# Backward pass of an attention and gated feed-forward block: one fixed use for each PSUM bank in the heads, places recomputed, and nine heads that make dV and dK in their stored layout

## Chip, core and metric

The kernel runs on one core of one Trainium2 chip. The metric is the device time of an execution in microseconds. A core has five engines that the text calls by these names: TensorE (PE in the profile; PEld is its weight load), VectorE (DVE), ScalarE (ACT), GpSimd (POOL) and SyncE (SP). Each engine works through its own instructions in order; matmuls write to PSUM, which has eight banks of 128 partitions x 512 f32 values. PSUM is emptied by VectorE or ScalarE. GpSimd and SyncE also issue the DMAs.

## The reference

The reference returns the output of a forward pass and its gradients (a vector-Jacobian product with grad_out). The forward pass, with S = 2048 rows, D = 576, 32 heads of size 128, F = 4608, all in bfloat16:

```
xn  = layernorm(x)
q   = (xn @ wq) by heads
p   = softmax(q @ k_cache^T / sqrt(128))        per head, 2048 x 2048
s   = concat_heads(p @ v_cache) @ wo
h   = sigmoid(xn @ w_gate) * (xn @ w_up)
g   = silu(h @ w_down)
out = x + s * g
```

Nine results are returned: out, dx, dK (out_2) and dV (out_3) of every head, dwq, dwo, dw_gate, dw_up, dw_down. For a head, with dO the gradient of its output, P the probabilities and delta the row sums of dO * O: dV = P^T dO, dS = P * (dO V^T - delta), dQ = dS K, dK = dS^T Q (with scales). dK and dV of a head are 2048 x 128.

## The kernel before

The kernel has stages that follow each other: layer norm and the feed-forward forward pass (to about 310 us), the down projection (to about 470 us), the 32 heads (to about 3680 us), the output projection (L851), the first feed-forward backward pass over 18 blocks of 256 of F's columns (L906 to L961), the gradients of wo and wq over 8 groups of heads (L1006, L1017), and the gradient of x (L1075).

**A head's work on TensorE.** The query rows come in 16 tiles (qt) of 128. For each qt and each half of the keys there are two 512-wide matmuls for the scores (s_half, L553) and later two for dP (dp_half, L586). VectorE takes the scores out with a running minimum (L555), ScalarE makes the unnormalised probabilities P (s_exp, L565), VectorE and ScalarE make dS (L589, L592, L596). SyncE issues transposing DMAs of pairs of P and dS tiles (trans_P, trans_dS). Then come the rows: for every qt 16 matmuls, 128 wide, of the transposed P with V (O, 256 per head) and of the transposed dS with K (dQ, 256 per head). Four qt make a group that fills one PSUM bank (row_mm, L617). A group of O is copied by ScalarE (o_sink: ou) and goes on to GpSimd (prod, o_n) and VectorE (delta); a group of dQ is copied by VectorE (dq_sink: dq_n, L680).

dV and dK are made in four passes per head (kv, kv_mm, L635): VA and VB give the halves of dV, KA and KB those of dK. A pass has 32 matmuls, 512 wide, and fills two banks with the result turned, head size on the partitions: the weights are a tile of dOn or Qn, the moving operand is a slab of P or dS. Each bank is copied by ScalarE (KVE = "ss") and stored by a GpSimd DMA to the scratch tensors dvT_d and dkT_d. dOn is the transposed dO, scaled in pairs of tiles by the reciprocal row sums (s_rinv on VectorE, s_scale on GpSimd, L573) once the exps of the pair are done; the first dV pass needs it.

Projections (proj, L510; 20 matmuls for QT of the next head, 20 for dOT) and transposes (pe_transposes, L517, in two groups of 8 each for KT, VT, dOn, Qn; prep_wo, five) fill one bank each and are copied by ScalarE or VectorE.

**Order.** A head has 64 places (HEAD). Every call is put into a list with a place by at(); the score and dP matmuls are anchors at the whole places (scores in 0 to 31, dP in 32 to 63). The list is sorted by place, and TensorE, VectorE and ScalarE get their instructions in that order. GpSimd's and SyncE's order is chosen when the kernel is built. Rows of group g start at place 13.6 + 8g (O) and 45.6 + 8g (dQ) and fill 8 places, so that groups follow each other directly; the places of the dV and dK passes come out of level(), which fills the places up to an equal load. They are 23.2 to 36.0 (VA), 37.4 to 53.2 (VB), 54.6 to 66.5 (KA) and 67.9 to 84.9 (KB); places over 64 lie in the next head.

**PSUM.** Score and dP matmuls use a pool of two buffers of two banks (ps_big). All else in the heads, rows, dV and dK passes, projections and transposes, shares one pool of four banks (ps_acc, tag "acc").

**Turns.** After the heads, dkT_d and dvT_d have to be turned: turn() issues on SyncE's queue a transposing DMA of 512 KB into SBUF and stores the tile that the turn before it brought (L156, L159). There are 64, one for each of dK and dV of each head: one in each block of the first feed-forward backward pass and one more in each odd block (27), two in each group of the next stage (16), and three in each of the last seven of eight blocks of the last (21).

Of the kernel before, what the change touches and what calls it, by code (L numbers as in the profile page):

```python
# [13 lines left out]
P = 128  # L14
# [81 lines left out]
def kernel(  # L96
# [47 lines left out]
    on2_d = dram.tile([S, HD], bf, name="on2_d")  # L144
    dq2_d = dram.tile([S, HD], bf, name="dq2_d")
    dkT_d = dram.tile([H, P, S], bf, name="dkT_d")
    dvT_d = dram.tile([H, P, S], bf, name="dvT_d")
    turns = [(src[h], out[0, h].rearrange("(p t) d -> p t d", t=NT)) for h in range(H) for src, out in ((dkT_d, out_2), (dvT_d, out_3))]
    turned = []
# [271 lines left out]
    with tc.tile_pool(name="ld2", bufs=2) as ld2, tc.tile_pool(name="ld1q", bufs=1) as ld1q, \  # L421
# [8 lines left out]
            tc.tile_pool(name="wh", bufs=2) as wh, tc.tile_pool(name="ld1", bufs=1) as ld1, \  # L430
            tc.tile_pool(name="ps_acc", bufs=4, space=PSUM) as ps_acc:

# [59 lines left out]
        def prep_wo(hs, eng):  # L492
            hs.woT = wh.tile([P, DT, P], bf, name="woT_h", bufs=1)
            nc.gpsimd.memset(hs.woT[:P - KL, DL, :], 0.0)
            pt = ps_acc.tile([P, 8, P], bf, name="acct", tag="acc")
            for j in range(DL):
                nc.tensor.transpose(pt[:, j, :], wo_h[:, j * P:(j + 1) * P], ident[:])
            nc.tensor.transpose(pt[:, DL, :], wo_h[:, D - P:D], ident[:])
            alt.copy(hs.woT[:, :DL, :], pt[:, :DL, :], eng=eng)
            alt.copy(hs.woT[P - KL:, DL, :], pt[P - KL:, DL, :], eng=eng)  # L500

        def proj(hs, name, c, i, eng):
            if c == 0 and i == 0:
                setattr(hs, name, ld1.tile([P, S], bf, name=name))
            w, srcT = (hs.wq, xnT) if name == "QT" else (hs.woT, dsT)
            cs = slice(c * CH, (c + 1) * CH)
            if i == 0:
                hs.acc_ = ps_acc.tile([P, CH], f32, name="accp", tag="acc")
            acc = hs.acc_
            nc.tensor.matmul(acc[:], lhsT=w[:, i, :], rhs=(srcT if i < DL else xnT)[:, i, cs], start=(i == 0), stop=(i == DL))  # L510
            if i == DL:
                alt.copy(getattr(hs, name)[:, cs], acc[:], eng=eng)

        def pe_transposes(src_fn, dst, g, eng):
            pt = ps_acc.tile([P, 8, P], bf, name="acct", tag="acc")
            for j in range(8):
                nc.tensor.transpose(pt[:, j, :], src_fn(g * 8 + j), ident[:])  # L517
            alt.copy(dst[:, g * 8:(g + 1) * 8, :], pt[:], eng=eng)
# [94 lines left out]
        def row_mm(bx, hs, T, rhs, qt, kt, sink):  # L613
            j = qt % GQ
            if j == 0 and kt == 0:
                bx.acc = ps_acc.tile([P, GQ, P], f32, name="acc", tag="acc")
            nc.tensor.matmul(bx.acc[:, j, :], lhsT=T[qt][:, kt, :], rhs=getattr(hs, rhs)[:, kt, :],  # L617
                             start=(kt == 0), stop=(kt == NT - 1))
            if j == GQ - 1 and kt == NT - 1:
                sink(bx.acc)  # L620

        def rows(pos, step, width, hs, T, rhs, g, sinks):
            bx = Box()
            sink, after = sinks
            for j in range(GQ):
                for kt in range(NT):
                    at(pos + step * j + width * kt / NT, row_mm, bx, hs, T, rhs, g * GQ + j, kt, sink)
            if after:
                at(pos + step * (GQ - 1) + width + AFTER, after)

        def kv_mm(bx, hs, slabs, rhs, half, qt, i, sink):
            if qt == 0:
                bx.acc[i] = ps_acc.tile([P, CH], f32, name="acckv", tag="acc")
            k0 = (half * 2 + i) * CH
            nc.tensor.matmul(bx.acc[i][:], lhsT=getattr(hs, rhs)[:, qt, :], rhs=slabs[qt][:, k0:k0 + CH],  # L635
                             start=(qt == 0), stop=(qt == NT - 1))
            if qt == NT - 1:
                sink(bx.acc[i], i)

        def kv(b, pos, hs, slabs, rhs, half, dst):  # L640
            bx = Box()
            bx.acc = [None, None]

            def sink(acc, i):
                c = half * 2 + i
                kv_t = stg.tile([P, CH], bf, name="kv", tag="stg", bufs=3)
                alt.copy(kv_t[:], acc[:], eng=KVE[i])
                nc.gpsimd.dma_start(dst[:, c * CH:(c + 1) * CH], kv_t[:])

            n = 2 * KPC  # L650
            for qt in range(NT):
                for i in range(2):
                    at(b + pos[qt * n + i * KPC], kv_mm, bx, hs, slabs, rhs, half, qt, i, sink)

# [31 lines left out]
        HEAD = 2 * H1  # L686
        XO, XQ = 13.6, 13.6
        KVE, OUE = "ss", "s"
        WOT_AT = 1.6
        QT_AT, DOT_AT = ((39.0, 47.2, 50.2, 56.4), "s"), ((7.8, 10.4, 16.2, 18.6), "s")  # L690
        KT_AT, DON_AT, VT_AT, QN_AT = (42.0, 43.6, "s"), (14.9, 24.4, "v"), (3.4, 26.4, "s"), (28.0, 32.2, "s")
        PSTEP = 0.4
        EXP_AT, RINV_AT, PT_AT, DST_AT, AFTER = 2.1, 4.6, 2.7, 2.0, 3.5

        KV0, KV1, GAP = 23.2, 85.9, 1.1
        BLK, WIDE = 1.0, CH / P
        load_ = [2 * WIDE + NT / 2] * (2 * HEAD)
        for p_ in (WOT_AT,):
            load_[int(p_)] += DT
        for ps_, n_ in [((KT_AT + DON_AT + VT_AT + QN_AT), 8)]:  # L700
            for p_ in ps_:
                if not isinstance(p_, str):
                    load_[int(p_)] += n_ * BLK
        for p_ in QT_AT[0] + DOT_AT[0]:
            for i in range(DT):
                load_[int(p_ + PSTEP * i)] += WIDE
        for k in range(HEAD):
            load_[HEAD + k] = load_[k]

        def level(top):  # L710
            out, pos, n = [], KV0, 2 * KPC * NT
            while pos < 2 * HEAD - 1 and len(out) < 4 * n:
                if len(out) % n == 0 and out:
                    pos += GAP
                k = int(pos)
                room = max(top - load_[k], 0.01)
                step = 1.0 / room
                out.append(pos)
                pos = min(pos + step, max(k + 1.0, pos + 1e-6)) if step > k + 1.0 - pos else pos + step
                if len(out) < n and len(out) % (2 * KPC) == 0:  # L720
                    pos = max(pos, 4.0 * (len(out) // (4 * KPC)) + 7.0)
            return out, pos

        lo_, hi_ = 10.0, 60.0
        for _ in range(60):
            mid = (lo_ + hi_) / 2
            o_, e_ = level(mid)
            if len(o_) < 4 * 2 * KPC * NT or e_ > KV1:
                lo_ = mid
            else:  # L730
                hi_ = mid
        kvpos = level(hi_)[0]
        assert len(kvpos) == 4 * 2 * KPC * NT
        VA, VB, KA, KB = (kvpos[2 * KPC * NT * k:2 * KPC * NT * (k + 1)] for k in range(4))
        WO_AT = 50.0
        MAN = {mybir.EngineType.PE, mybir.EngineType.DVE, mybir.EngineType.Activation}
        for h in range(H):
            hs = Head(h)
            b = h * HEAD
            back = lambda x: b - HEAD + x if h else b - 14 + x / 8  # L740
            at(back(35.0), load_w, hs)
            at(back(35.1), load_kv, hs)
            for c in range(NCH):
                for i in range(DT):
                    at(back(QT_AT[0][c] + PSTEP * i), proj, hs, "QT", c, i, QT_AT[1])
                    at(b + DOT_AT[0][c] + PSTEP * i, proj, hs, "dOT", c, i, DOT_AT[1])
            at(b + WOT_AT, prep_wo, hs, "s")
            for g in range(2):
# [17 lines left out]
            for g in range(NG):  # L766
                rows(b + 8 * g + XO, 2, 2, hs, hs.PT, "Vn", g, o_sink(hs, g))
                rows(b + H1 + 8 * g + XQ, 2, 2, hs, hs.dST, "Kn", g, dq_sink(hs, g))
            for half, (pv, pk_) in enumerate(((VA, KA), (VB, KB))):
                kv(b, pv, hs, hs.P, "dOn", half, dvT_d[h])  # L770
                kv(b, pk_, hs, hs.dS, "Qn", half, dkT_d[h])
        bl = (H - 1) * HEAD
# [15 lines left out]
    if True:  # L788
# [79 lines left out]
        FB = min(256, F)  # L868
        with tc.tile_pool(name="b1o", bufs=2, reuse_waits="tile") as outp, tc.tile_pool(name="b1k", bufs=3, reuse_waits="tile") as tkp, tc.tile_pool(name="b1t", bufs=3, reuse_waits="tile") as tmpp, \
                tc.tile_pool(name="b1r", bufs=2, reuse_waits="tile") as dblk, \  # L870
# [20 lines left out]
            for fb in range(F // FB):  # L891
                if fb % 2:
                    turn(tkp)
                fcols = slice(fb * FB, (fb + 1) * FB)
# [147 lines left out]
        with tc.tile_pool(name="c4c", bufs=1, reuse_waits="tile") as chp, tc.tile_pool(name="c4s", bufs=2, reuse_waits="tile") as sb, \  # L1042
# [11 lines left out]
            for sbi in range(S // SB2):  # L1054
# [7 lines left out]
                for pi, (src_d, wT, k0, KC, nm) in enumerate(passes):  # L1062
                    ch = chp.tile([P, KC, SB2], bf, name=f"cq{pi % 2}" if nm == "cq" else f"cf{pi % 3}")
                    nc.sync.dma_start_transpose(ch[:], src_d[scol, k0 * P:(k0 + KC) * P])
                    if sbi == 0 and pi in (1, 3, 4, 6):
                        load_wqT((1, 3, 4, 6).index(pi))
                    elif sbi and pi % 3 == 1:
                        turn(tkp)
# [67 lines left out]
```

## Time and profile before

| | us |
|---|---|
| three timed runs | 5139.92, 5182.06, 5144.55 |
| median of these | 5144.55 |
| the profiled execution, its own time | 5156.55 |
| its span, first to last instruction | 5154.8 |
| one head, from one wait of TensorE to the same wait in the next (1977.44 to 2077.06) | 99.6 |

| busy in a stretch of 100 us | TensorE | VectorE | ScalarE | GpSimd |
|---|---|---|---|---|
| 2000 to 2100 us (heads) | 96.8 | 81.7 | 64.5 | 32.9 |
| 4100 to 4200 us (first feed-forward backward pass) | 88.2 | 24.7 | 19.6 | 27.7 |
| 4900 to 5000 us (gradient of x) | 99.2 | 12.6 | 3.6 | 4.3 |

A view of the profile is of one execution. A line of the timeline gives the start, the duration, the engine, the line of the kernel, the operation with its operands (written <- read), the shapes, how many like it were merged, and in brackets the idle time before it with what ended it. A line of the view of waits gives who waited for whom, the total, how often, and the longest. Some matmul records are missing from the trace. Matmuls are pipelined: the next starts before the last has ended, so the issue rate is read from start to start.

### The profile page before, as it was taken

The page shows a single profiled execution, that of the slowest core. Times are in us where ns is not written, and L with a number is a line of the kernel's source. Part 1 is how long each engine was busy: PE and PEld are TensorE (multiplying, and loading weights), DVE is VectorE, ACT ScalarE, POOL GpSimd, SP SyncE. Part 2 cuts the span into 40 slices and gives each one's busy share as a digit, 9 for nine tenths or more (in the row PEclk, how much of TensorE's full clock was granted, in tenths as well). Part 3 has the DMA queues.
Part 4 walks back from the last instruction along what each step waited for, and adds up shares of the span by engine and source line. Part 5 has one row for each costly group of instructions (what it writes and reads, how often), then busy time and mean ns, then how long its engine had stood idle before and what let it go on. Part 6 is the DMA issues. An engine that isn't in the chain of part 4 may idle for free.

```text
span 5154.8 us, 100626 instructions
## 1 busy us (share of the span) xinstructions
PE 4926.1 (96%) x41765; PEld 3051.4 (59%) x42512; DVE 3157.1 (61%) x4789; ACT 2415.2 (47%) x3099; POOL 1479.5 (29%) x2197
## 2 busy tenths in 40 slices
PE   9999999999999999999999999999888999998999
PEld 3344666666666666666666566666547778754554
DVE  6545888888888888888888788888432222110101
ACT  5533656666665665666666566656201222100000
POOL 4322332332333333233333323332212233211000
PEclk9999999999999999999999999999999999999999
DMA  7876999999999999999999999999999999999998
GB/s 263 256 210 149 202 208 201 204 207 201 206 202 204 204 204 206 205 203 205 207 202 202 199 202 204 204 202 217 201 208 224 223 242 239 281 266 242 208 206 183
DMA packets 2905211, 1095.60 MB, mean 213 GB/s; under 512 B 2710064, under 2 KB 2832944, under 8 KB 2904752
## 3 DMA queue, kind: packets, MB, share of 16 engines
q1 hardware_dynamic: 2819488, 803.33, 87.4%
q0 software_dynamic: 85264, 285.79, 20.4%
q8 instruction: 332, 5.44, 0.4%
q14 instruction: 127, 1.04, 0.1%
HBM read 172.54 MB, written 234.55 MB: 79 GB/s over the span
## 4 chain that ended last, share of the span: by engine, by line
PE 76%; DMA 7%; issue 6%; DVE 5%; ACT 5%; POOL 1%; SPq 1%; ACTq 0%; DVEq 0%; POOLq 0%; another core or an unknown queue 0%
PE acc L617 14%; PE acckv L635 13%; PE acc L1075 8%; PE dp L586 7%; PE sp L553 6%; PE accp L510 5%; PE accw L948 4%; DVE sneg L555 3%; PE acc L391 3%; PE dh L906 2%; PE accd L924 2%; PE acc L1006 2%; PE accq L1017 2%; DMA b_blk<-b_d 2%; PE acc L851 2%
## 5 line engine op out<-in xcount | busy, mean ns | idle before, releaser
L565 ACT ACTIVATE Pq<-sneg,nm 128x2048 bf16<-128x2048 bf16 x512 | 1026.7, 2005 | 158.9 <-DVE sneg L555 156.2
L617 PE MATMUL acc<-Kn,dST 128*128 128x128 bf16 x8192 | 1034.5, 219 | 28.3 <-DMA dST<-dSq 16.7
L589 DVE SCALAR_TENSOR_TENSOR dSq<-dp,delta,Pq 128x1024 bf16<-128x1024 f32 x608 | 773.2, 1281 | 378.8 <-PE dp L586 377.2
L617 PEld LDWEIGHTS <-dST 128*128 128x128 bf16 x8192 | 713.8, 98 | 466.8 <-issue 28.0
L617 PE MATMUL acc<-Vn,PT 128*128 128x128 bf16 x8192 | 947.3, 219 | 30.1 <-ACT dOT L40 15.5
L617 PEld LDWEIGHTS <-PT 128*128 128x128 bf16 x8192 | 680.2, 98 | 417.0 <-issue 25.4
L635 PE MATMUL acckv<-dSq,Qn 128*128 128x512 bf16 x1915 | 707.5, 380 | 23.1 <-ACT kv L40 22.1
L635 PE MATMUL acckv<-Pq,dOn 128*128 128x512 bf16 x1892 | 701.0, 380 | 26.5 <-POOL dOn L573 22.8
L555 DVE TENSOR_SCALAR_CACHE_REDUCE sneg<-sp 128x1024 bf16<-128x1024 f32 x512 | 625.4, 1222 | 143.6 <-PE sp L553 90.8
L555 DVE TENSOR_SCALAR_CACHE_REDUCE sneg<-sp,nm 128x1024 bf16<-128x1024 f32 x512 | 656.8, 1283 | 74.2 <-PE sp L553 48.0
L592 ACT ACTIVATE t<-dp,negdelta 128x1024 bf16<-128x1024 f32 x416 | 464.2, 1116 | 454.4 <-PE dp L586 288.7
L553 PE MATMUL sp<-KT,QT 128*128 128x512 bf16 x1985 | 597.9, 380 | 7.0 <-DVE sneg L555 6.7
L586 PE MATMUL dp<-VT,dOT 128*128 128x512 bf16 x1913 | 580.4, 379 | 1.8 <-DVE dSq L589 1.0
L596 DVE TENSOR_TENSOR dSq<-t,Pq 128x1024 bf16<-128x1024 bf16 x416 | 407.4, 979 | 0.0
L635 PEld LDWEIGHTS <-dOn 128*128 128x128 bf16 x2048 | 200.6, 98 | 99.0 <-POOL dOn L573 34.6
L1088 DVE SCALAR_TENSOR_TENSOR junk<-dxn,xn_all 128x576 f32<-128x576 f32 x16 | 12.1, 758 | 381.3 <-ACT dxn L1083 381.3
L510 PE MATMUL accp<-xnT,wq_h 128*128 128x512 bf16 x639 | 241.2, 382 | 3.5 <-ACT xnT L40 0.8
L635 PEld LDWEIGHTS <-Qn 128*128 128x128 bf16 x2048 | 200.7, 98 | 72.7
L948 PEld LDWEIGHTS <-xn_all 128*128 128x128 bf16 x2304 | 224.1, 98 | 30.6 <-issue 2.8
L1075 PEld LDWEIGHTS <-cf 128*128 128x128 bf16 x2304 | 147.6, 99 | 154.3 <-DMA cf<-du_d 7.5
L573 POOL TENSOR_TENSOR dOn<-dOn,rinv_all 128x256 bf16<-128x256 bf16 x256 | 153.9, 610 | 204.8 <-DVE rinv_all L569 147.0
L1083 ACT ACTIVATE dxn<-acc 128x512 f32<-128x512 f32 (+1 forms) x32 | 12.8, 406 | 413.6 <-issue 344.3
(182 smaller groups left out, 6983.4 us busy)
## 6 DMA issues: line engine op xcount, KB each, us to landing
out_dram<-turn SPq DMA_DIRECT2D x64, 512.0 KB, 4.5
h_d<-h_row POOLq DMA_DIRECT2D x48, 384.0 KB, 3.0
a_d<-a_row POOLq DMA_DIRECT2D x48, 384.0 KB, 3.4
b_d<-b_row POOLq DMA_DIRECT2D x48, 384.0 KB, 4.5
a_blk<-a_d SPq DMA_DIRECT2D x18, 1024.0 KB, 13.2
b_blk<-b_d SPq DMA_DIRECT2D x18, 1024.0 KB, 18.9
du_d<-du_blk POOLq DMA_DIRECT2D x18, 1024.0 KB, 9.4
dg_d<-dg_blk POOLq DMA_DIRECT2D x18, 1024.0 KB, 12.8
```

The lines of the kernel that those rows point to most:

```text
L510: nc.tensor.matmul(acc[:], lhsT=w[:, i, :], rhs=(srcT if i < DL else xnT)[:, i, cs], start=(i == 0), stop=(i == DL))
L553: nc.tensor.matmul(sp[:, c * CH:(c + 1) * CH], lhsT=hs.QT[:, qs], rhs=hs.KT[:, hf * HW_ + c * CH: hf * HW_ + (c + 1) * CH], start=True, st ...
L555: nc.vector.tensor_scalar(sneg[:, hf * HW_:(hf + 1) * HW_], sp[:], -SCALE, None if hf == 0 else nm[:, hf - 1:hf], op0=ALU.mult, op1=ALU.mi ...
L565: nc.scalar.activation(Pq, sneg[:], AF.Exp, bias=nm[:, hf:hf + 1], scale=-1.0, accum_out=hs.rs_all[:, qt:qt + 1])
L586: nc.tensor.matmul(dp[:, c * CH:(c + 1) * CH], lhsT=hs.dOT[:, qs], rhs=hs.VT[:, hf * HW_ + c * CH: hf * HW_ + (c + 1) * CH], start=True, s ...
L589: nc.vector.scalar_tensor_tensor(dSq[:, hsl], dp[:], hs.delta[:, qt:qt + 1], Pq[:, hsl], op0=ALU.subtract, op1=ALU.mult)
L592: nc.scalar.activation(t[:], dp[:], AF.Identity, bias=hs.negdelta[:, qt:qt + 1], scale=1.0)
L596: nc.vector.tensor_tensor(dSq[:, hsl], t[:], Pq[:, hsl], op=ALU.mult)
L617: nc.tensor.matmul(bx.acc[:, j, :], lhsT=T[qt][:, kt, :], rhs=getattr(hs, rhs)[:, kt, :], start=(kt == 0), stop=(kt == NT - 1))
L635: nc.tensor.matmul(bx.acc[i][:], lhsT=getattr(hs, rhs)[:, qt, :], rhs=slabs[qt][:, k0:k0 + CH], start=(qt == 0), stop=(qt == NT - 1))
L948: nc.tensor.matmul(acc[:kd, :FB], lhsT=xn_all[:, st, d0:d0 + kd], rhs=blk_[:, st, :], start=(st == 0), stop=(st == NT - 1))
L1075: nc.tensor.matmul(accs[sl][j][:, :nn], lhsT=ch[:, kk, sl * P:(sl + 1) * P], rhs=w_[:, n0:n0 + nn], start=(pi == 0 and kk == 0), stop=(las ...
```

## The change

Three things are changed.

1. The pool of four banks is split: two banks for the dV and dK passes (ps_kv), one for the rows (ps_row), one for projections and transposes (ps_tr).
2. The places are new. A row group fills 7.1 of its 8 places, from 14.8 + 8g (O) and 46.8 + 8g (dQ), which leaves 0.9 places until the next. The four passes now lie at 23.0 to 36.9 (VA), 38.5 to 52.2 (VB), 53.2 to 70.1 (KA) and 71.1 to 86.0 (KB). Projections, transposes, the load of the weights of the next head and prep_wo move, as the diff shows, and level() loads the first half of the places 3% over, the second half 3% under the mean. The first bank of each pass is now copied by VectorE (KVE = "vs").
3. Heads 0 to 8 (STORED = 9) make dV and dK as they are stored, keys on the partitions: four 128-wide matmuls with a piece of the slab as weights take the place of each 512-wide one. They go to out_2 and out_3 directly, and 18 turns are left out: those of the odd blocks of the first feed-forward backward pass, and nine of the last stage, which now has two in each of six blocks. The pool of turned tiles in the first of these has two buffers in place of three.

```diff
-    turns = [... for h in range(H) for src, out in ((dkT_d, out_2), (dvT_d, out_3))]
+    STORED = 9
+    turns = [... for h in range(STORED, H) for src, out in ((dkT_d, out_2), (dvT_d, out_3))]
...
-            tc.tile_pool(name="ps_acc", bufs=4, space=PSUM) as ps_acc:
+            tc.tile_pool(name="ps_kv", bufs=2, space=PSUM) as ps_kv, \
+            tc.tile_pool(name="ps_row", bufs=1, space=PSUM) as ps_row, \
+            tc.tile_pool(name="ps_tr", bufs=1, space=PSUM) as ps_tr:
...
-        def rows(pos, step, width, hs, T, rhs, g, sinks):
+        def rows(pos, hs, T, rhs, g, sinks):
...
-                    at(pos + step * j + width * kt / NT, row_mm, bx, hs, T, rhs, g * GQ + j, kt, sink)
+                    at(pos + ROW_W * (j * NT + kt) / (GQ * NT - 1), row_mm, bx, hs, T, rhs, g * GQ + j, kt, sink)
             if after:
-                at(pos + step * (GQ - 1) + width + AFTER, after)
+                at(pos + ROW_W + AFTER, after)
...
         def kv_mm(bx, hs, slabs, rhs, half, qt, i, sink):
             if qt == 0:
-                bx.acc[i] = ps_acc.tile([P, CH], f32, name="acckv", tag="acc")
+                bx.acc[i] = ps_kv.tile([P, CH], f32, name="acckv")
             k0 = (half * 2 + i) * CH
-            nc.tensor.matmul(bx.acc[i][:], lhsT=getattr(hs, rhs)[:, qt, :], rhs=slabs[qt][:, k0:k0 + CH],
-                             start=(qt == 0), stop=(qt == NT - 1))
+            w = getattr(hs, rhs)[:, qt, :]
+            if hs.h < STORED:
+                for j in range(KPC):
+                    nc.tensor.matmul(bx.acc[i][:, j * P:(j + 1) * P], lhsT=slabs[qt][:, k0 + j * P:k0 + (j + 1) * P], rhs=w,
+                                     start=(qt == 0 and j == 0), stop=(qt == NT - 1 and j == KPC - 1))
+            else:
+                nc.tensor.matmul(bx.acc[i][:], lhsT=w, rhs=slabs[qt][:, k0:k0 + CH], start=(qt == 0), stop=(qt == NT - 1))
...
-                nc.gpsimd.dma_start(dst[:, c * CH:(c + 1) * CH], kv_t[:])
+                if hs.h < STORED:
+                    nc.gpsimd.dma_start(out[0, hs.h].rearrange("(p t) d -> p t d", t=NT)[:, c * KPC:(c + 1) * KPC, :],
+                                        kv_t[:].rearrange("p (t d) -> p t d", d=P))
+                else:
+                    nc.gpsimd.dma_start(turned_d[hs.h][:, c * CH:(c + 1) * CH], kv_t[:])
...
-        XO, XQ = 13.6, 13.6
-        KVE, OUE = "ss", "s"
-        WOT_AT = 1.6
-        QT_AT, DOT_AT = ((39.0, 47.2, 50.2, 56.4), "s"), ((7.8, 10.4, 16.2, 18.6), "s")
-        KT_AT, DON_AT, VT_AT, QN_AT = (42.0, 43.6, "s"), (14.9, 24.4, "v"), (3.4, 26.4, "s"), (28.0, 32.2, "s")
+        XR, ROW_W = 14.8, 7.1
+        KVE, OUE = "vs", "s"
+        WOT_AT = 57.0
+        QT_AT, DOT_AT = ((33.0, 45.6, 54.0, 61.3), "s"), ((2.2, 5.9, 13.6, 18.7), "s")
+        KT_AT, DON_AT, VT_AT, QN_AT = (37.2, 40.5, "s"), (9.0, 22.2, "v"), (0.4, 10.4, "s"), (24.6, 28.2, "s")
...
-        KV0, KV1, GAP = 23.2, 85.9, 1.1
+        KV0, GAP = 23.0, 0.7
+        WIDE, TILT = 3.88, 0.03
...
-                if len(out) < n and len(out) % (2 * KPC) == 0:
-                    pos = max(pos, 4.0 * (len(out) // (4 * KPC)) + 7.0)
+                if n < 2 * NT:
+                    pos = max(pos, 4.0 * (n // 4) + 7.7, DON_AT[1] + 2.0 if n >= NT else 0.0)
...
-            at(back(35.0), load_w, hs)
+            at(back(20.0), load_w, hs)
...
-            at(b + WOT_AT, prep_wo, hs, "s")
+            at(back(WOT_AT), prep_wo, hs, "s")
...
-                if fb % 2:
-                    turn(tkp)
...
-                    elif sbi and pi % 3 == 1:
+                    elif sbi and sbi < NSB - 1 and pi % 4 == 1:
                         turn(tkp)
```

back(x) is place x of the head before; for the first head, place -14 + x / 8.

## The prediction

> **What bounds the kernel now.** I began with the page: busy shares, then the slices.
>
> ```profile
> span 5154.8 us, 100626 instructions
> PE 4926.1 (96%) x41765; PEld 3051.4 (59%) x42512; DVE 3157.1 (61%) x4789; ACT 2415.2 (47%) x3099; POOL 1479.5 (29%) x2197
> ```
>
> TensorE is busy for all but 229 us, so any gain lies in its idle time, or comes from giving it less work. The slices put the 32 heads at about 480 to 3680 us. Next, who TensorE waits for between 500 and 3600 us (total, times, longest):
>
> ```profile
> PE acckv L635 <- POOL dOn L573: 22.8, 31, 0.8
> PE acckv L635 <- ACT kv L40: 22.1, 31, 0.7
> PE acc L617 <- ACT dOT L40: 15.0, 30, 0.8
> PE acct L517 <- ACT VT L40: 12.1, 31, 0.5
> PE acc L617 <- DMA dST<-dSq: 5.8, 4, 3.2
> ```
>
> Four waits, once per head each. Three are for the copy out of a PSUM bank that something else used before; one is for the scaling of dOn by GpSimd. The timeline of TensorE in the head from 1970.87 us shows three of them and the issue rate (start, duration, matmuls merged, wait before):
>
> ```profile
> 2004.54 0.39 PE L617 MATMUL acc<-Vn,PT 128*128 128x128 bf16 x4
> 2005.42 0.38 PE L617 MATMUL acc<-Vn,PT 128*128 128x128 bf16 x4 [0.49 <-ACT dOT L40]
> ...
> 2006.07 0.61 PE L617 MATMUL acc<-Vn,PT 128*128 128x128 bf16 x8
> 2006.52 0.59 PE L553 MATMUL sp<-KT,QT 128*128 128x512 bf16 x2
> 2006.95 0.22 PE L617 MATMUL acc<-Vn,PT 128*128 128x128 bf16 x1
> ...
> 2015.04 0.61 PE L517 MATMUL acct<-ident,QT 128*128 128x128 bf16 x8 [0.27 <-ACT VT L40]
> ...
> 2026.53 0.39 PE L635 MATMUL acckv<-Pq,dOn 128*128 128x512 bf16 x1 [0.62 <-POOL dOn L573]
> ```
>
> Eight 128-wide matmuls, each with its own weight load, take 0.45 us (56 ns each); two 512-wide take 0.43 (216 ns each). Counted by starts (four matmuls from 2004.54 end issuing at 2004.76, the next starts at 2005.42) the four waits are 0.66, 0.43, 0.78 and, at 1977.44, 0.88: 2.75 us of a head of 99.6 us. Without them it takes 96.9 us, 1.51 us per place (64 places).
>
> After the heads I read the first feed-forward pass (L906 on) on TensorE and SyncE's queue:
>
> ```profile
> 3967.66 5.61 PE L906 MATMUL dh<-wdT,doBT 128*128 128x256 bf16 x30 [8.08 <-ACT dhc L910]
> 4109.76 6.22 PE L906 MATMUL dh<-wdT,doBT 128*128 128x256 bf16 x30 [9.69 <-ACT dhc L910]
> ```
>
> ```profile
> 3896.08 24.98 SPq L156 DMA_TRANSPOSE turn<-dkT_d  x1
> 3921.15 16.67 SPq L156 DMA_TRANSPOSE turn<-dvT_d  x1
> ...
> 3941.86 0.56 SPq L884 DMA_DIRECT2D a_blk<-a_d  x1
> ```
>
> dhc waits for VectorE, and that for a_blk and b_blk, whose loads stood behind two turns on SyncE's queue. From 4190 us on TensorE is over 99% busy there, and again from 4780 us.
>
> **The change, part by part.** *Old waits.* Fixed banks and new places remove the three bank waits; the fourth, for dOn, is moved. 31 x 2.75 = 85 us is the most that the heads can give: -85.
>
> *New waits.* Each bank has one user now, so its hole must cover the copy on an engine that works in order. The code's levelling gives places of the first half 3% more work than the mean, those of the second half 3% less: 1.56 and 1.47 us. A row group's hole is 0.9 places long: it runs from 0.9 to 1.8 places after the start of the place in which the group ends.
>
> Rows of dQ, copied by VectorE. In the second half the group now ends at place 53.9:
>
> ```profile
> 2054.77 1.28 DVE L589 SCALAR_TENSOR_TENSOR dSq<-dp,delta,Pq 128x1024 bf16<-128x1024 f32 x1 [1.46 <-PE dp L586]
> 2055.97 0.68 DVE L596 TENSOR_TENSOR dSq<-t,Pq 128x1024 bf16<-128x1024 bf16 x1
> 2056.57 0.68 DVE L680 TENSOR_TENSOR dq_n<-acc,rsc 128x512 bf16<-128x512 f32 x1
> ```
>
> The matmul of place 53 started at 2054.14, the copy ends at 2057.25, 3.1 us later. VectorE's order stays; the next group starts 1.8 x 1.47 = 2.65 us after place 53: wait 0.5 (0.4 to 0.7). The group ending at 61.9 has 2.5 us against 2.65: none. The group ending at 5.9: dq_n ended 2.54 us after place 5 (1979.23 to 1981.77), but now a dK bank whose last matmul is at 5.7 is copied by VectorE just before it (0.6; an f32 512-wide copy has a mean of 691 ns): 3.15 against 1.8 x 1.56 = 2.8: wait 0.4 (0.2 to 0.6). At 13.9 dq_n ended after 2.54: none.
>
> Rows of O, copied by ScalarE behind an exp (2.0 us) or, at 37.9, behind the KT copy (1.0), now at 37.2. At 29.9 the copy ended 3.0 us after place 29 (2016.14 to 2019.16), with 2.8 to come: 0 to 0.5 each, together 0.5 (0 to 1.0).
>
> dOn pair 7 moves from 35.0 to 35.7, 1.03 us, past its old 0.78: 0.2 (0 to 0.5). Pair 6 comes earlier: its first matmul (the 25th of the first dV pass) falls at 31.7, before at 33.4. Its scaling ended at 2023.2, place 33.4, because GpSimd's queue held prod, o_n and a store issue in front:
>
> ```profile
> 2019.24 1.15 POOL L663 TENSOR_TENSOR prod<-ou,dOn 128x512 f32<-128x512 bf16 x1 [0.57 <-ACT ou L40]
> 2020.35 1.04 POOL L670 TENSOR_TENSOR o_n<-ou,rinv_all 128x512 bf16<-128x512 bf16 x1
> 2021.68 0.82 POOL L671 DMA_DIRECT2D on_d<-o_n  x1 [0.29 <-POOL o_n L670]
> 2022.53 0.63 POOL L573 TENSOR_TENSOR dOn<-dOn,rinv_all 128x256 bf16<-128x256 bf16 x1
> ```
>
> If that order stays and ou is a little later, the wait is 1.3 places, 2.0 us; if the scaling goes first (its reciprocal ended at 2020.03, place 31.4), 0.15. No view shows the new order: the middle, 1.0. Transposes and projections share one bank; the tightest pair, dOn at 9.0 and VT at 10.4, leaves 2.2 us for 0.67 of transposes, up to 1.28 of VectorE's current work and 0.68 of copy: 0.2 (0 to 0.46). The dV/dK passes have holes of 1.05 to 1.7 places for 0.6 us copies: 0.1 (0 to 0.6).
>
> Together 2.9; a wait gives the other engines time for the next, so I take 2.5 (0.75 to 5.9): x32, +80.
>
> *Stored heads.* 128 of these matmuls per head, nine heads: 1,152 become four each. 4 x 56 - 216 = 8 ns: +9 us. Stores keep 128 runs of 1 KB: nothing.
>
> The Trainium skill speaks against this part ("TensorE: Matmul & The Clock Gate", "Back-to-back issue gap"): in a real stream of weight load and matmul it gives about 81 ns per 128-wide and about 131 ns per 512-wide matmul. By that the nine heads would cost an estimated 1,152 x (324 - 131) = 222 us, and the sum would come out near 5345. Here the eight in a row disagree (56 ns, 216 ns).
>
> *Start.* Before the first score matmul, four QT chunks, two KT groups and one woT now pass through one bank. Each waits its copy (QT 0.58 mean, KT 1.0) and 0.22 of drain: about 7 x 0.95 = +6.5 once (0 to 8).
>
> *Row transposes.* Rows start 1.2 places later after the same transposing DMAs: of the 5.8 us of waits half goes, -3 (0 to -6). Earlier weight loads queue on GpSimd, already counted as its order.
>
> *Turns.* 18 of 64 go: nine at odd blocks of the first feed-forward pass, nine in the last stage. The second of the turns above held the loads for 20 us, more than the 8.08 wait; the 9.69 and a 1.76 at 4179.5 follow pairs of turns too: -19.5 (-5 to -28, all waits there). In the last stage TensorE's 99% hides turns: 0; should that cover fail, a turn's 3 us issue is the price. A last store still closes the kernel: 0.
>
> Sum: -85 + 80 + 9 + 6.5 - 3 - 19.5 = -12 us. The profiled execution took 5156.55 (span 5154.8), so 5144.5 against it; the median of the three runs, 5144.55, lies 12 lower, and I forecast against the median: 5132.
>
> **The rivals.** *All holes hold.* New waits are only 0.3 us per head: -85 + 10 + 9 + 6.5 - 3 - 19.5 = -82, 5062. For it: ScalarE is 65% and GpSimd 33% busy in the heads, and pair 6 may be scaled first. Against: the 3.1 us at place 53.
>
> *The single row bank.* All four dQ copies, on a VectorE that is 82% busy in the heads and takes four more copies per head, come 0.8 us late, as place 53's would behind one more VectorE step: 3.2 + 0.5 + 1.0 + 0.15 = 4.85 per head, 155 for 80: +63, 5207. It decides where a copy ends over 0.9 places after its group. For it: place 53. Against: 2.5 us at places 13 and 61.
>
> *Weight loads bind.* If four loads of 98 ns no longer hide in long 128-wide stretches: 4 x 98 - 216 = 176 ns, 203 us for 9: 5326. Against: 56 ns over eight; no longer run at full clock shows it.
>
> **How the numbers follow.** Forecast 0.52; all holes 0.24; row bank 0.19; weight loads 0.05. A change under about 1% (51 us) is what a measurement can't tell from none. Faster takes the second case and an edge of the first, 0.26; slower the last two less an edge, 0.22; within, 0.52. The range takes in the centres of both neighbours, 5060 to 5207; the forecast's own is 5095 to 5170.
>
> **What would show it.** Right: TensorE's waits for kv, dOT and VT gone; waits of L617 for dq_n near places 54 and 6 in their stead, and of the dV matmuls for dOn at 31.7; the first nine heads about 1 us longer than the rest; no 8 or 10 us waits at L906. Wrong: heads under 98 us, or over 101, or 128-wide matmuls in stored heads far from 56 ns.

## The result, and the profile after

The changed kernel takes 5204.41 us (median of 20 runs, 5175.03 to 5218.51); the kernel before, run beside it, 5142.24 us (20 runs, 5121.87 to 5188.17). The ratio, taken over all runs and not from the two medians, is 1.0109, 95% interval 1.0087 to 1.0130: slower by 1.1%, where 5132 us and no change had been forecast. The profiled execution of the changed kernel took 5175.03 us, the fastest of its 20 runs, 29 us under the median; it is only 18 us over the profiled execution of before, and the rest of the difference has to be looked for in what varies from run to run.

The page of the changed kernel begins:

```profile
span 5173.1 us, 107352 instructions
PE 4946.6 (96%) x45178; PEld 3197.5 (62%) x45968; DVE 3162.0 (61%) x4917; ACT 2354.6 (46%) x2971; POOL 1481.8 (29%) x2197
```

More TensorE instructions (the stored heads), and the same share of idle time. Who TensorE waits for in the heads, 500 to 3650 us (total, times, longest):

```profile
PE acckv L644 <- POOL dOn L576: 48.4, 39, 2.1
PE acckv L641 <- POOL dOn L576: 18.7, 18, 1.9
PE acc L620 <- DVE dq_n L691: 17.8, 57, 0.4
PE acc L620 <- DMA dST<-dSq: 11.8, 7, 2.9
PE acc L620 <- ACT ou L40: 10.2, 31, 0.3
```

The waits for kv and VT are gone and that for dOT is left in one head, as forecast; but the wait for dOn, 0.8 us at most before, is now about 2 us in every head. L641 is the stored form of a dV matmul and L644 the other; both wait for the same scaling. GpSimd's timeline in the head that spans 3100.93 to 3201.66 us shows what stands in front of that scaling:

```profile
3175.82 1.16 POOL L674 TENSOR_TENSOR prod<-ou,dOn 128x512 f32<-128x512 bf16 x1 [3.54 <-ACT ou L40]
3176.94 1.04 POOL L681 TENSOR_TENSOR o_n<-ou,rinv_all 128x512 bf16<-128x512 bf16 x1
3178.27 0.82 POOL L682 DMA_DIRECT2D on_d<-o_n  x1 [0.29 <-POOL o_n L681]
3179.12 0.62 POOL L576 TENSOR_TENSOR dOn<-dOn,rinv_all 128x256 bf16<-128x256 bf16 x1
```

The order is that of before: prod, o_n, the store's issue, then pair 6's scaling. It ends at 3179.74, and the 25th matmul of the first dV pass, which comes up on TensorE before that, starts at 3179.80 after 2.09 us of wait:

```profile
3177.38 0.33 PE L620 MATMUL acc<-Vn,PT 128*128 128x128 bf16 x3
3179.80 0.39 PE L644 MATMUL acckv<-Pq,dOn 128*128 128x512 bf16 x1 [2.09 <-POOL dOn L576]
```

Most heads that nothing else disturbs take one of three times in the changed kernel. First two heads of before, then three of after, from GpSimd's load of one Vn to the next (window, its length, busy time of each engine, granted clock, share of DMA time, GB/s):

```profile
1044.56:1143.92 99.36, 96.25 (x863) 61.45 (x878) 82.40 (x115) 64.05 (x74) 33.15 (x47) 1.00 1.15 209
2541.16:2640.78 99.62, 96.09 (x862) 61.53 (x878) 81.39 (x115) 64.15 (x74) 32.90 (x47) 1.00 1.15 204
```

```profile
1056.05:1157.43 101.38, 97.28 (x1242) 77.67 (x1262) 81.82 (x119) 62.22 (x70) 33.01 (x48) 1.00 1.19 204
3302.40:3403.12 100.72, 96.57 (x862) 61.45 (x878) 81.77 (x119) 62.20 (x70) 33.00 (x48) 1.00 1.15 206
1566.02:1668.42 102.40, 98.25 (x862) 62.21 (x878) 81.78 (x119) 62.20 (x70) 33.02 (x48) 0.98 1.12 196
```

The first of after is a stored head, the second an unstored one, 1.1 us longer than before. The third is unstored too and has the same 2.09 us wait, yet takes 1.7 us more, and its granted clock is 0.98 (three more heads at 0.98 take 102.04 to 102.06, 1.3 us more). Finer windows show where. In the changed kernel's record of the clock every change lies on one grid of 3.413 us, which runs on through the whole kernel. Two stretches of that grid around the wait in a head that drops, then in the head of 3179.80 that does not, each with the stretch that follows:

```profile
1539.53:1542.94 3.41, 1.32 (x13) 0.80 (x13) 1.43 (x5) 0.90 (x2) 2.58 (x4) 1.00 1.06 197
1542.94:1546.35 3.41, 3.41 (x18) 1.78 (x16) 0.00 (x0) 2.35 (x2) 0.00 (x0) 0.50 1.10 203
...
3177.90:3181.31 3.41, 1.51 (x13) 0.93 (x14) 0.42 (x2) 0.42 (x1) 1.52 (x3) 1.00 1.14 207
3181.31:3184.73 3.42, 3.42 (x35) 2.24 (x34) 2.32 (x3) 3.41 (x4) 0.00 (x0) 1.00 0.39 84
```

Where all of the wait falls into one stretch, TensorE is busy for 1.32 us of it, idle for 2.09, and the whole next stretch runs at a clock of 0.50: half of 3.41 us, up to 1.7 us, is lost. Where the grid cuts the wait, the stretch has 1.51 us busy, 1.90 idle, and the next one runs at full clock.

After the heads, the first FF-backward pass no longer waits for its inputs. The longest wait for dhc was 9.7 us there before, 22.7 us in all; between 3650 and 4600 us it is now:

```profile
PE dh L923 <- ACT dhc L927: 1.5, 2, 1.3
```

### The profile page after: what moved, and what is told of

The parts are those of the page before. It is cut to its first block, busy times and chain, and to the rows that moved or that the text cites. A ratio compares the mean times of both kernels' runs of the same rounds, so it can differ in the third digit from the quotient of the medians.

```text
span 5173.1 us, 107352 instructions
## 1 busy us (share of the span) xinstructions
PE 4946.6 (96%) x45178; PEld 3197.5 (62%) x45968; DVE 3162.0 (61%) x4917; ACT 2354.6 (46%) x2971; POOL 1481.8 (29%) x2197
## 4 chain that ended last, share of the span: by engine, by line
PE 75%; issue 7%; DVE 6%; DMA 5%; POOL 3%; ACT 2%; another core or an unknown queue 1%; SPq 1%; DVEq 0%; ACTq 0%; POOLq 0%
PE acc L620 13%; PE acckv L644 8%; PE acc L1092 7%; PE dp L589 6%; PE sp L556 5%; PE accw L965 5%; PE accp L513 4%; PE acckv L641 4%; PE dh L923 3%; DVE sneg L558 3%; PE acc L392 3%; PE accd L941 3%; PE acc L870 2%; PE g_ps L295 2%; PE acc L1023 2%
## 5 line engine op out<-in xcount | busy, mean ns | idle before, releaser
L620 PE MATMUL acc<-Kn,dST 128*128 128x128 bf16 x8192 | 941.3, 219 | 41.3 <-DVE dq_n L691 19.1
L620 PE MATMUL acc<-Vn,PT 128*128 128x128 bf16 x8192 | 927.8, 220 | 32.1 <-DMA PT<-Pq 10.5
L620 PEld LDWEIGHTS <-dST 128*128 128x128 bf16 x8192 | 660.5, 98 | 370.9 <-issue 29.5
L620 PEld LDWEIGHTS <-PT 128*128 128x128 bf16 x8192 | 659.6, 99 | 350.3 <-issue 30.4
L644 PE MATMUL acckv<-Pq,dOn 128*128 128x512 bf16 x1401 | 522.3, 384 | 52.2 <-POOL dOn L576 49.8
L644 PE MATMUL acckv<-dSq,Qn 128*128 128x512 bf16 x1379 | 517.5, 380 | 1.9
L599 DVE TENSOR_TENSOR dSq<-t,Pq 128x1024 bf16<-128x1024 bf16 x416 | 332.3, 799 | 0.0
L576 POOL TENSOR_TENSOR dOn<-dOn,rinv_all 128x256 bf16<-128x256 bf16 x256 | 156.9, 613 | 356.8 <-DVE rinv_all L572 206.4
L641 PE MATMUL acckv<-dOn,Pq 128*128 128x128 bf16 x2304 | 216.2, 219 | 20.1 <-POOL dOn L576 18.7
L641 PE MATMUL acckv<-Qn,dSq 128*128 128x128 bf16 x2304 | 220.7, 219 | 2.5
L674 POOL TENSOR_TENSOR prod<-ou,dOn 128x512 f32<-128x512 bf16 x128 | 153.6, 1200 | 212.5 <-ACT ou L40 211.0
L644 PEld LDWEIGHTS <-dOn 128*128 128x128 bf16 x1472 | 145.2, 99 | 112.0 <-POOL dOn L576 56.9
```

The lines of the kernel that those rows point to most:

```text
L599: nc.vector.tensor_tensor(dSq[:, hsl], t[:], Pq[:, hsl], op=ALU.mult)
L641: nc.tensor.matmul(bx.acc[i][:, j * P:(j + 1) * P], lhsT=slabs[qt][:, k0 + j * P:k0 + (j + 1) * P], rhs=w, start=(qt == 0 and j == 0), sto ...
L644: nc.tensor.matmul(bx.acc[i][:], lhsT=w, rhs=slabs[qt][:, k0:k0 + CH], start=(qt == 0), stop=(qt == NT - 1))
```

## The experiments

The theory: the change is slower for one wait, pair 6's, which is long because of GpSimd's order and the new place, and which costs twice: its length, and the half-clock stretch that it sets off where about 2 us of it fall into one stretch of the grid. Rivals: the wait costs only its length and the rest is elsewhere (the stored form, the turns, the shorter holes); the place and not the queue is the cause; when it is removed, another wait takes its place. All ratios stand to the kernel before, run beside each on the same chip; "half clock" is the time at half clock among the heads of the profiled execution, from the trace's record of the granted clock (17 us for the kernel before, 51 us for the change). In every kernel 7 to 24 us of it lie at the start of the heads, before 500 us.

| kernel | median us | ratio (95% interval) | wait for dOn, longest | half clock, us |
|---|---|---|---|---|
| the change | 5204.41 | 1.0109 (1.0087 to 1.0130) | 2.1 | 51 |
| pair6_late | 5115.82 | 0.9959 (0.9930 to 0.9988) | 0.1 | 7 |
| on_by_vector | 5198.87 | 1.0121 (1.0080 to 1.0163) | 2.2 | 106 |
| on_off_queue | 5129.91 | 0.9981 (0.9958 to 1.0005) | 0.7 | 20 |
| pair6_bit | 5174.78 | 1.0076 (1.0043 to 1.0108) | 2.0 | 61 |
| pair6_past_dp | 5150.11 | 1.0038 (1.0017 to 1.0058) | 1.4 | 24 |
| stored_alone | 5123.23 | 0.9970 (0.9942 to 0.9998) | 0.8 | 14 |
| none_stored | 5221.74 | 1.0183 (1.0154 to 1.0213) | 2.1 | 89 |
| late_none | 5119.53 | 0.9998 (0.9967 to 1.0029) | 0.1 | 7 |
| all_stored | 5110.39 | 0.9955 (0.9932 to 0.9978) | none | 27 |
| late_hole | 5117.15 | 0.9970 (0.9948 to 0.9992) | none | 20 |

**pair6_late: the wait taken away by place.** In the levelling:

```diff
-                    pos = max(pos, 4.0 * (n // 4) + 7.7, DON_AT[1] + 2.0 if n >= NT else 0.0)
+                    pos = max(pos, 4.0 * (n // 4) + 7.7 + (2.5 if n // 4 == 6 else 0.0), DON_AT[1] + 2.0 if n >= NT else 0.0)
```

> The last eight matmuls of the first dV pass start at place 34.2 instead of 31.7, past the end of pair 6's scaling. Theory: the wait for dOn of 1.9 to 2.1 us per head is gone and nothing comes in its place: 32 x 2.0 = 64 us, and the half-clock stretches behind it (10 to 20 of 1.7 us): 5100 to 5125 us, clock 0.994 or above. Rival (the work that now stands later takes a wait of its own, for a slab or at the end of the pass): 5170 us or more, with another name on the wait.

Measured 5115.82 us, 0.9959 (0.9930 to 0.9988): 1.5% below the change and under the kernel before. TensorE's waits in its heads (500 to 3540 us):

```profile
PE acc L620 <- DVE dq_n L691: 24.0, 29, 0.8
PE acc L620 <- ACT ou L40: 10.2, 31, 0.3
PE acckv L644 <- ACT kv L40: 7.7, 22, 0.4
PE acct L520 <- DVE dOn L42: 6.6, 30, 0.2
```

No wait of GpSimd is among them. Others grew a little (dq_n from 16.8 us in the same window to 24.0, kv and dOn's bank from nothing to 0.2 to 0.4 a head), and a quiet head takes 99.05 us for 100.73: 1.7 us of the wait's 2.1 come back, and the half-clock time with it (mean clock of all runs 0.9933, of the change 0.9894). 1.7 us in 32 heads are 54 us, and half of the 44 us less at half clock are 22: together 76 us, the 1.5%. The theory stands; the rival of another wait in its place holds for about a fifth of it.

**on_by_vector and on_off_queue: the wait taken away by queue, all places left.** The second group's o_n goes to VectorE, and in the second kernel its store to SyncE as well:

```diff
-                nc.gpsimd.tensor_tensor(o_n[:], ou[:], bcast(hs.rinv_all[:, gs], GQ), op=ALU.mult)
+                (nc.vector if g == 1 else nc.gpsimd).tensor_tensor(o_n[:], ou[:], bcast(hs.rinv_all[:, gs], GQ), op=ALU.mult)
...
-                nc.gpsimd.dma_start(on2_d[...], o_n[:])
+                (nc.sync if g == 1 else nc.gpsimd).dma_start(on2_d[...], o_n[:])
```

> The second group's o_n is made by VectorE instead of GpSimd; no place is changed. GpSimd's queue then holds only the product ahead of pair 6's scaling, and the store's issue behind it. Theory (queue order is the cause): the scaling comes about 2.1 us sooner, the wait for dOn falls below 0.3 us, and the time to 5105 to 5135 us, VectorE's extra 0.3 to 0.6 us per head lying beside TensorE. Rival (the place is the cause: the exponentials and reciprocals of tiles 12 and 13 are not done before): the wait stays near 2 us and the time at about 5204 us.

The time did not move: 5198.87 us, 1.0121 (1.0080 to 1.0163). But GpSimd's timeline shows that pair 6 was cured (the first L576) and that the wait had moved to pair 7 (the second); VectorE's rows stand below it:

```profile
2564.87 1.16 POOL L674 TENSOR_TENSOR prod<-ou,dOn 128x512 f32<-128x512 bf16 x1 [3.54 <-ACT ou L40]
2566.09 0.61 POOL L576 TENSOR_TENSOR dOn<-dOn,rinv_all 128x256 bf16<-128x256 bf16 x1
2571.94 0.59 POOL L680 TENSOR_SCALAR negdelta<-delta 128x4 f32<-128x4 f32 x1 [5.23 <-DVE delta L679]
2572.74 0.82 POOL L682 DMA_DIRECT2D on_d<-o_n  x1 [0.21 <-DVE rinv_all L572]
2573.59 1.18 POOL L576 TENSOR_TENSOR dOn<-dOn,rinv_all 128x256 bf16<-128x256 bf16 x1
```

```profile
2571.77 0.68 DVE L681 TENSOR_TENSOR o_n<-ou,rinv_all 128x512 bf16<-128x512 bf16 x1
2572.37 0.15 DVE L572 RECIPROCAL rinv_all<-rs_all 128x2 f32<-128x2 f32 x1
```

Pair 6 is scaled 0.06 us after prod, so the queue had been the cause there and its reciprocals were in time. The store's issue, which needs the o_n that VectorE ends at 2572.45, now stands in front of pair 7's scaling. The reciprocal for it is there at 2572.52, itself 0.6 us later as o_n stands ahead of it on VectorE; the scaling starts at 2573.59, takes 1.18 us where 0.6 is usual (why, no run shows) and ends at 2574.77. The 2.2 us wait is the old one at the next pair. It drops the clock in 25 of the heads, from 1449 to 3190 us in every one, 106 us at half clock:

```profile
1773.47:1875.83 102.36, 98.25 (x862) 62.20 (x878) 80.83 (x120) 62.29 (x70) 32.83 (x46) 0.98 1.10 199
1875.83:1978.19 102.36, 98.25 (x862) 62.25 (x878) 80.83 (x120) 62.29 (x70) 32.84 (x46) 0.98 1.08 200
```

That is 102.36 / 3.413 = 30.0 stretches of the grid: a head that drops is just long enough for the next head's wait to fall on the same spot of the grid, so that it drops as well. An undisturbed head of the change, 100.73 us, is 29.5 stretches and leaves the spot again.

> The kernel on_by_vector, whose wait for dOn had moved from pair 6 to pair 7 (2.2 us, behind the store's issue that waits for VectorE's o_n), with this one store of each head issued by SyncE instead of GpSimd. All places are those of the changed kernel. Theory (GpSimd's queue is the cause, and a wait under 1.95 us leaves the clock alone): pair 7's scaling comes 1.1 to 1.5 us sooner, the wait falls to 0.6 to 1.1 us, half-clock time among the heads to 20 us or less: 5199 - 32 x 1.3 - 40 = 5118 us (5105 to 5140). Rival (the store, waiting on SyncE's queue, holds up the row transposes behind it): waits for PT and dST in most heads and above 5160 us.

5129.91 us, 0.9981 (0.9958 to 1.0005), with every place as in the change. The waits of its heads (500 to 3540 us):

```profile
PE acc L620 <- DVE dq_n L691: 17.1, 54, 0.6
PE acckv L644 <- POOL dOn L576: 14.5, 22, 0.7
...
PE acckv L641 <- POOL dOn L576: 5.9, 9, 0.7
```

Two thirds of the dOn wait are gone, the half-clock time is 20 us, and SyncE's transposes were not held up (dST 7.1 us, 11.8 in the change). It is the queue that makes the place bad: a later place (pair6_late) takes 1.5% off, a freed queue 1.3%.

**pair6_bit and pair6_past_dp: the wait made shorter.** The same line of the levelling with 0.2 and with 0.4 in place of 2.5.

> The 25th matmul of the first dV pass is put 0.2 of a place later (at 31.9), behind three O matmuls and one pair of dP matmuls, about 0.6 us of TensorE work; nothing else is moved. Theory (clock): the wait for dOn shrinks from 2.1 us to about 1.5 us, and as no stretch of 3.413 us then holds 2 us of idle TensorE, no half-clock stretch follows it in any head: 32 x 0.6 = 19 us less wait, and 10 to 20 half-clock stretches of 1.7 us less, so about 5150 us (5140 to 5165), mean granted clock 0.994 or above. Rival (a wait costs its length alone): 19 us off 5204, about 5185 us, clock as in the changed kernel.

The edit was misjudged: two 128-wide matmuls went ahead instead of 0.6 us of work, and the wait only fell to 1.98 us, 1.8 in stored heads. 5174.78 us, 1.0076 (1.0043 to 1.0108), with 61 us at half clock in the profiled execution. As the wait hardly moved, the run can't tell the two theories apart; it shows that 1.97 to 1.98 us are still enough to drop the clock.

> The same edit as pair6_bit, which passed only two 128-wide matmuls and took 0.1 us off the wait, now with 0.4 of a place: the 25th matmul of the first dV pass is passed by four O matmuls and the pair of dP matmuls, 0.65 us, so the wait for dOn is about 1.4 us. Theory (clock, sharper after the first runs: a 3.413 us stretch with about 1.95 us or more of idle TensorE is followed by one at half clock): no head is followed by a half-clock stretch; 32 x 0.65 = 21 us of wait and the 50 to 60 us at half clock among the heads, half of which is lost time, 25 to 30 us: 5150 to 5165 us, clock 0.994 or above. Rival (the wait costs its length alone): about 5183 us, clock 0.989 to 0.990.

5150.11 us, 1.0038 (1.0017 to 1.0058); the waits of its heads (500 to 3540 us):

```profile
PE acckv L644 <- POOL dOn L576: 29.7, 21, 1.4
...
PE acckv L641 <- POOL dOn L576: 11.2, 9, 1.3
```

The wait is 0.65 us shorter, 21 us over 32 heads; by the ratios the kernel is 36 us faster than the change (by the medians 54, but the kernel before ran 5.5 us faster beside it). By its length alone the ratio would be 1.0068, which lies outside the interval. As both ratios have an interval, the margin is thin, but the clock speaks for the same: no wait for dOn is followed by half clock here. Time at half clock in the profiled execution fell from 51 to 24 us; 7 us of what is left are at the start, four of the five other stretches follow waits for row transposes (2.1 to 3.9 us) and one a 2.0 us wait for an exp. Over all runs the mean clock is 0.9933, for 0.9894 in the change: 40 us less at half clock, so 20 us, which with the 21 us make 41. A wait of 2.1 us costs more than one of 1.4 by more than the difference of their lengths.

**stored_alone, none_stored, late_none: the two halves apart.** stored_alone is the kernel before with STORED = 9, the four narrow matmuls in kv_mm, the store straight to the output and the turns as in the change. none_stored is the change with these taken back (the third buffer for turned tiles too):

```diff
-    STORED = 9
+    STORED = 0
...
+                if fb % 2:
+                    turn(tkp)
...
-                    elif sbi and sbi < NSB - 1 and pi % 4 == 1:
+                    elif sbi and pi % 3 == 1:
```

late_none is pair6_late with the same lines taken back.

> The kernel before with the other half of the change alone: the first nine heads make dV and dK as stored, no turn is issued in the first FF-backward pass, the dX passes turn at every fourth chunk. Banks and places as before. Theory: the five waits of the first FF-backward pass (22.7 us) and the 3.1 and 2.2 us waits beside them are gone, and the half-clock stretches behind two of them (six of 3.413 us, 10 us); the nine heads cost 0.7 to 1.0 us more each: 5142 - 28 - 10 + 8 = 5112 us (5100 to 5125). Rival as forecast: only the 19.5 us of two passes' waits, 5131 us. Rival (the stored form upsets the shared banks): above 5142 us.

> The changed kernel with banks, places and holes alone: no head makes dV or dK as stored, all 64 turns stand where they stood before. Theory: the stored heads' 7 us and the turns' 13 to 20 us come back with opposite signs, and 1.7 us per tripped head may come on nine heads more, whose wait is then 2.1 us instead of 1.9: 5204 - 7 + 20 + 7 = 5224 us (5205 to 5240). Rival (the stored form and the turns are what lost the time): 5160 us or below.

> The kernel pair6_late without the other half of the change: no head makes dV or dK as stored, all 64 turns stand where they stood before. Banks, places and holes stay, and no wait is near 1.95 us, so the clock is out of play. Theory (the two halves add): the nine heads give back 9 x 0.83 = 7 us, the turns of the first FF-backward pass cost 20 us and more: 5116 + 13 = 5129 us (5120 to 5140), clock 0.993 or above; the unstored heads run at 99.05 us, which against 99.62 before is what banks, places and holes are worth without their wait. Rival (the halves hang together, as the stored heads relieve the banks): beyond 5145 us or below 5112 us.

stored_alone: 0.9970 (0.9942 to 0.9998), 5123.23 us for 5136.23 us, 13 us less. That is 11 us short of the expected 5112; the forecast's 10.5 us of gain (19.5 less 9) was nearer. One stall that the profile puts down to no one was left in the first FF-backward pass of this execution:

```profile
PE dh L914 <- issue: 10.1, 2, 7.4
```

none_stored: 5221.74 us, 1.0183 (1.0154 to 1.0213), as expected. So banks, places and holes alone lose 1.8%, and the stored heads and turns win a part of it back. It is 0.7%, more than the 0.3% that they win in stored_alone. A stored head's wait is 1.90 us and drops the clock in none of the seven undisturbed ones, an unstored one's 2.09 often does: none_stored spends 89 us at half clock, the change 51, and half of these 38 us is the missing 0.4%.

late_none: 0.9998 (0.9967 to 1.0029). With the wait gone, banks and places alone stand level with the kernel before, within 0.3%, and the other half is worth 0.4% on top of it (0.9998 to 0.9959) and 0.3% by itself (0.9970): without the clock the halves add, as far as intervals of 0.3% on each ratio let one say. (The kernel before ran at 5121.63 us beside late_none, so only the ratios compare.)

**all_stored and late_hole: two terms of the forecast in pair6_late.** STORED = 32 in the first; ROW_W = 6.7 for 7.1 in the second.

> The kernel pair6_late with all 32 heads storing dV and dK as made, so that no turn is left. It prices the stored form: the profile's nine heads cost 0.83 us each more than the others in pair6_late (99.88 against 99.05). Theory: 23 x 0.83 = 19 us more in the heads, and less than 10 us back in the last passes, where turns stand behind full buffers: 5116 + 19 - 5 = 5130 us (5120 to 5140). Rival (the turns collide with the last passes' own transposes): below 5105 us.

5110.39 us, 0.9955 (0.9932 to 0.9978), against 0.9959 for pair6_late: no difference to be told. A stored head takes 99.88 us and an unstored one 99.05 in pair6_late, so 23 more cost 19 us (all_stored's undisturbed heads do take 99.88). The medians would have the passes after the heads give about as much back, more than the 5 us of the theory, less than the rival's 30; but in the two profiled executions they take only 9 us less, 1574 us from the last load of Vn to the end for 1583. How the rest came back stays open.

> The kernel pair6_late with the O and dQ groups packed into 6.7 places instead of 7.1, so that the hole after each is 1.3 places (2.0 us) instead of 0.9 (1.4 us). Theory: the waits for dq_n (0.8 us per head) and ou (0.33) are the hole's being too short and go: 32 x 1.1 = 35 us at most, 5080 to 5095 us. Rival (dq_n stands behind other work on VectorE and comes late by more than the hole gains, or denser rows find their transposes not landed): 5110 us or more.

5117.15 us, 0.9970 (0.9948 to 0.9992): nothing gained, as the rival had it. The wait for dq_n is 1.0 us in 21 heads, for 0.8 in 29 of pair6_late, and that for ou rises from 0.3 to 0.6; dST's waits went from 5.2 to 22.0 us. This fits copies that come when VectorE and ScalarE get to them and not when the group ends, but no row here shows it directly.

## Why the prediction was wrong, step by step

Counted as the prediction counted (from the time at which the matmul before could have handed over to the start of the next), a quiet unstored head of the change idles 4.03 us where the forecast had 2.5. Four of the five waits, in the order of time (the fifth, pair 6, is shown above):

```profile
3113.67 0.22 PE L620 MATMUL acc<-Kn,dST 128*128 128x128 bf16 x1 [0.21 <-DVE dq_n L691]
...
3138.51 0.27 PE L620 MATMUL acc<-Kn,dST 128*128 128x128 bf16 x2 [0.41 <-DVE dq_n L691]
...
3185.83 0.39 PE L644 MATMUL acckv<-Pq,dOn 128*128 128x512 bf16 x1 [0.18 <-POOL dOn L576]
...
3190.49 0.27 PE L620 MATMUL acc<-Vn,PT 128*128 128x128 bf16 x2 [0.33 <-ACT ou L40]
```

The brackets count from the modelled end of the matmul before; by starts the waits are 0.37, 0.57, 0.34 and 0.50 us.

- *Old waits, 2.75 us a head, gone:* right. kv and VT do not return, dOT in one head.
- *dQ rows, 0.5 near place 54 and 0.4 near place 6:* 0.37 and 0.57, right in sum and put down to dq_n, with the larger at the other place. That a longer hole does not remove them, late_hole shows.
- *O rows, 0.5:* 0.50, one wait behind the KT copy. *dOn pair 7, 0.2:* 0.34. *VT in the shared bank, 0.2, and kv holes, 0.1:* none.
- *dOn pair 6, 1.0, the middle of 0.15 and 2.0:* 2.25. **This is the step that failed.** The prediction had both ends and the right reason for the high one ("if that order stays"), and took the middle since no view showed the new order. The order stayed, and GpSimd's rows of before, which showed it, were the nearest evidence there was. A middle between two outcomes was a value that neither gives. The high end was short too: its own rows, scaling done at place 33.4 and matmul at 31.7, are 1.7 places or about 2.6 us apart, not 1.3 places and 2.0 us.
- *Less 0.4 for sharing:* nothing was shared, the five waits lie 4.7 us and more apart.

Together 1.53 us a head, 49 us over 32 heads: -12 becomes +37. The other part is a term that the sum did not have, **the clock**: 51 us at half clock among the heads for 17 before, so 17 us lost in the profiled execution. It also accounts for much of the distance from that execution to the median: the 20 runs' mean clocks lie between 0.992 (5175 and 5190 us) and 0.987 (5216 and 5219 us), and a mean clock lower by 0.005 is 0.010 of 5200 us more at half clock, 52 us, of which 26 are lost.

The Trainium skill has the rule that was missing ("TensorE: Matmul & The Clock Gate", "What's actually happening"): the clock falls to half after an idle window of about 3.4 us, and the windows run freely, 3413 ns each. The grid and the half agree with the trace (0.50, 3.413 us). The threshold does not: by the same page's "HAM oscillation — how this bites in real kernels" a gap must pass some 3.4 us, and 2.09 us sufficed here.

- *Stored heads, +9:* +0.66 us each in the change, +0.83 in pair6_late, so 6 to 7.5 us: right, and with them the 56 ns. The 222 us that the prediction estimated from the Trainium skill ("TensorE: Matmul & The Clock Gate", "Back-to-back issue gap") did not come; all_stored has 32 such heads and is no slower.
- *Start, +6.5:* the first head took 105.78 us for 98.89, 6.9 more, but 1.1 of it is what every head lost and 1.7 is half clock (17.1 us there for 13.7): about 4 is left, inside its range of 0 to 8; that 6.9 stands so near to 6.5 is luck. *Row transposes, -3:* 16.4 us of dST and PT waits for 5.8; wrong in sign in this execution, though pair6_late has 6.2 with the same row places, so more likely chance than place. *Turns, -19.5, last stage 0:* the 8 and 10 us waits went; with the stored heads 13 us by stored_alone, for -10.5. The 0 for the last stage stays open: all_stored, with no turn left, won back 9 us after the heads in its profiled execution and some 20 by the medians, with an interval of 12 us to either side.
- Of the rivals, "all holes hold" (5062) is ruled out even with pair 6 cured, at 0.9959; "the single row bank" named the right side and a number close by (5207), but its mechanism, all four dQ copies 0.8 late, is not there: dq_n takes 0.94 us a head. "Weight loads bind" is out.
- Of the signs, "heads over 101 us" was the one that spoke: 102.40, and 101.38 in the stored ones.

## What to carry to other kernels

When a matmul is moved ahead in a hand-made order, read the queue of the engine that it waits for and price the wait at that queue's present order, all of it, as a forecast of its own and not as a middle. Look at how much of the waiting falls into one short stretch and not at a head's sum: here four waits of 0.4 to 0.9 us, spread over a head, left the clock alone, and one of 2.1 us cost up to 1.7 us on top. A cure that moves work off a queue can leave another entry there that waits for the moved work, as the store's issue did.

## What the hardware showed that was not expected

In the twelve profiles of this study, between 500 and 5100 us, some 170 stretches of the 3.413 us grid at full clock were followed by one at half clock, and in each of them TensorE idled at least 0.56 of the time; of the stretches with a full-clock successor the idlest idled 0.59. The edge thus lies between about 1.9 and 2.0 us of idle time in one stretch, whether in one wait or in several (in late_hole 1.40 and 0.75 us in one stretch were enough). Nothing here shows why it lies there.

And the grid can lock a loop: a period of 102.36 us, 30.0 stretches, repeated the drop head after head in on_by_vector, which would not have shown in a price per wait.
